# Retention and two gated layers on one core: Lo parts of x and the first twelve weight tiles' additions moved from VectorE to GpSimd

## The chip, the cores and the metric

The kernel runs on one core of a Trainium2 chip. Its engines are TensorE (PE, with PEld for its weight loads), VectorE (DVE), ScalarE (ACT), GpSimd (POOL) and SyncE (SP), which issues most DMAs. Each engine works through its own instructions in order and waits on semaphores for the others. The metric is the device time of one execution in microseconds; less is better.

## What is computed

Retention over 4 batches, 8 heads, 576 positions and head size 64, then a layer with a clipped square, then a layer with a product of two branches:

```python
scores = scale * np.matmul(q, k.transpose(0, 1, 3, 2))
ret = scores * Dmat[None]            # Dmat: gamma ** (i - j) below the diagonal
x = np.matmul(ret, v)                # to 2304 tokens x 512
h = x @ moe_w_in                     # 512 x 2048
g = np.where(h >= 1, h, np.where(h <= -1, 0.0, (h + 1) ** 2 / 4))
x = g @ moe_w_out                    # 2048 x 512
out = ((x @ w_a) * (x @ w_b)) @ w_out  # 512 x 1536, 512 x 1536, 1536 x 512
```

The weights are float64 in memory.

## The kernel before

Most matmuls take operands in a 32-bit form of their own (float32r). To keep accuracy, x, g and every weight tile are held as two parts: Hi is a copy in that form, made by ScalarE, and Lo is the difference between the value and Hi, made by VectorE. A product is three matmuls, Hi by Hi, Hi by Lo, Lo by Hi (`HL`).

The retention runs in 36 units u, two for each chunk of 128 tokens. A unit's data come by one DMA from SP (L379) into a tile `u`, of which four exist, so unit u's load waits until unit u - 4 has been used by TensorE. GpSimd multiplies its values by a decay (L387) and, for a chunk in which a sequence begins, clears a part (L390, memset). TensorE makes scores (`s`), VectorE masks them (`retf`, L417), TensorE makes the output (`po`) and the state (`pn`), VectorE scales the output into `xf` (L481), ScalarE copies Hi into `x` (L486) and VectorE writes Lo into `x` (L487). The first 14 units use plain float32 operands; the later ones are split in Hi and Lo as well (`z` L395/L396, `ret` L425/L426, `st` L472/L473).

Six units make one block of 384 tokens. From block 0 on, the first layer runs in steps: a step is a column chunk f of w_in (`ph`, twelve matmuls of 128x384, L523 on), the activation (`act1`: `t` L535 to L537, `g` L541/L542) and the product with the row chunk f of w_out into four accumulators (`acc`). While block b runs its steps, one unit or more of block b + 1 is done in each step. Steps go in three groups of chunks (`GROUPS1`); in the first group block 0 uses chunks 0 to 3 and blocks 1 to 5 use 0 to 5, so that twelve weight tiles, w_in and w_out of chunks 0 to 5, are needed there. The groups' sums are stored (`yst`, L577, by VectorE and ScalarE in turn, then a DMA from SP) and added to later. x is stored too (`xd`, L939), by SP.

A weight tile comes as raw 64-bit words (`raw`, L140, by SP's queue until about 84 us, by GpSimd's after that) and is converted in place of a cast: two ScalarE instructions (L152, L153), a shift (L154), a merge of the sign (L157) and an integer addition (L160) on VectorE give `conv`. Then `split` (L163) writes Hi (L165, ScalarE) and Lo (L166, VectorE) into `w`. `conv` has two buffers, `raw` three and one more in the early part. `made[0]` counts the tiles of the first layer that are done, 32 in all.

The program is recorded in source order, and a scheduler then sets the order of each engine's instructions by a timeline of its own. So an edit to a few lines can move others on every engine. The second layer (`qx`, `qy`, `qz`, `late`) converts its weights by the same functions, with `made[0]` past 12.

Of the kernel before, what the change touches and what calls it, by code (L numbers as in the profile page):

```python
# [9 lines left out]
F32 = mybir.dt.float32  # L10
# [5 lines left out]
ALU = mybir.AluOpType  # L16
# [9 lines left out]
    [(0, 4)] + [(0, 6)] * (NB1 - 1), [(4, 11)] + [(6, 11)] * (NB1 - 1), [(11, 16)] * NB1  # L26
]
WHOLE = 14
NF2 = 12
HT = 384  # L30
WBUFS, WBUFS2 = 17, 1
# [50 lines left out]
def retention_ffn_kernel(  # L82
# [12 lines left out]
    nc = tc.nc  # L95
# [31 lines left out]
    def col_chunk(w, f):  # L127
        return w[:, f * P:(f + 1) * P].rearrange("(c p) f -> p c f", p=P)
# [14 lines left out]
    def convert(raw, t=None):  # L143


        w = raw.bitcast(U32).rearrange("p (n t) -> p t n", t=2)
        low, high = w[:, 0, :], w[:, 1, :]
        r = raw.bitcast(I32).rearrange("p (n t) -> p t n", t=2)[:, 0, :]
        if t is None:
            t = cpool.tile([P, 512], F32, tag="conv", name="conv")  # L150
        tu, ti = t.bitcast(U32), t.bitcast(I32)
        nc.scalar.activation(t, high.bitcast(F32), AF.Abs, scale=2.0 ** -112)  # L152
        nc.scalar.activation(r, low, AF.Copy, scale=2.0 ** -29)  # L153
        nc.vector.tensor_scalar(  # L154
            out=tu, in0=tu, scalar1=3, scalar2=None, op0=ALU.logical_shift_left
        )
        nc.vector.scalar_tensor_tensor(  # L157
            out=tu, in0=high, scalar=0x80000000, in1=tu, op0=ALU.bitwise_and, op1=ALU.bitwise_or
        )
        nc.vector.tensor_tensor(out=ti, in0=ti, in1=r, op=ALU.add)  # L160
        return t

    def split(t, pool):  # L163
        wt = pool.tile([P, 2, 512], F32R, tag="w", name="w")
        nc.scalar.copy(wt[:, 0, :], t)  # L165
        nc.vector.tensor_sub(wt[:, 1, :], t, wt[:, 0, :].bitcast(F32))  # L166
        return wt


# [10 lines left out]
    second = []  # L180
    for p in range(NF2 // 2):
        if p == LEAD:
            second += [row_chunk(w_out2, f) for f in range(2)]
        second += [col_chunk(w, 2 * p + j) for w in (w_a, w_b) for j in range(2)]
    second += [row_chunk(w_out2, f) for f in range(2, NF2)]
    weights, home = {}, {}
    room = {"w": [wpool, WBUFS]}
    made = [0]
# [55 lines left out]

    qd = [[dpool.tile([P, 2, 512], F32, name=f"q{p}_{k}") for k in range(7)] for p in range(NF2 // 2)]
    od = [[dpool.tile([P, 2, 512], F32, name=f"o{j}_{r}") for r in range(NF2 // 4)] for j in range(7)]
    A11, A12, A21, A22, S1, S2, S3, S4 = range(8)
# [3 lines left out]
    def maker():  # L251

        for p in range(NF2 // 2):
            if p == LEAD:
                yield from last_tiles(0, 2)
            tiles = {}
            for w in range(2):
# [24 lines left out]
                yield  # L282
        yield from last_tiles(2, NF2)

# [96 lines left out]
    def prepare(u):  # L381
# [7 lines left out]
        if more:  # L389
            nc.gpsimd.memset(t[0:r0, R0:V0], 0.0)  # L390
        if u < WHOLE:
            units[u, "z"] = t.unsqueeze(1)
# [8 lines left out]
    def passes(u):  # L401

        return HL[:1] if u < WHOLE else HL

    def score(u):
# [14 lines left out]
        )  # L420
        if u < WHOLE:
            rets[u] = f.unsqueeze(1)
# [10 lines left out]
    def output(u):  # L433
        c, d = divmod(u, 2)
        z, r = units[u, "z"], rets.pop(u)
# [5 lines left out]
        for e in range(2):  # L441
# [6 lines left out]
            for r0, _, m in inter:  # L448
                st = state[d].unsqueeze(1) if u < WHOLE else split_state[d]
                for n, (a, b) in enumerate(hl):  # L450
# [6 lines left out]
        if s0 + m < S:  # L457
# [10 lines left out]
            else:  # L468
                nc.vector.tensor_add(st, pn[:, 0:2 * P], st)
            if u + 2 >= WHOLE:  # L470
                h = split_state[d] = a2.tile([P, 2, 2 * P], F32R, tag=f"st{d}", name="st")
# [5 lines left out]
        fv = f.rearrange("p (c i) -> p c i", c=2)  # L477
# [6 lines left out]
            )  # L484
        xs = x[:, :, 2 * d:2 * d + 2, o]
        cast[0] = nc.scalar.copy(xs[:, 0], fv)  # L486
        nc.vector.tensor_sub(xs[:, 1], fv, xs[:, 0].bitcast(F32))  # L487
        del units[u, "z"]

    masked, cast = [None], [None]  # L490
# [584 lines left out]
```

## Time and profile before

| what | us |
|---|---|
| median of 3 runs | 926.08 (924.2 to 927.02) |
| the profiled execution | 925.54 |
| its span, first to last instruction | 923.8 |
| TensorE busy in it | 906.6 |
| VectorE busy | 662.0 |
| ScalarE busy | 486.3 |
| GpSimd busy | 69.9 |

TensorE's mean granted clock is 0.995 of 2.4 GHz. Busy times are sums over the span; the share of an engine differs much between the early part, where weights are converted and units run beside the first layer, and the rest. A matmul's row lists a duration that overlaps its neighbours', since they are pipelined; the pace is the difference between starts.

### The profile page before, as it was taken

The page shows a single profiled execution, that of the slowest core. Times are in us where ns is not written, and L with a number is a line of the kernel's source. Part 1 is how long each engine was busy: PE and PEld are TensorE (multiplying, and loading weights), DVE is VectorE, ACT ScalarE, POOL GpSimd, SP SyncE. Part 2 cuts the span into 40 slices and gives each one's busy share as a digit, 9 for nine tenths or more (in the row PEclk, how much of TensorE's full clock was granted, in tenths as well). Part 3 has the DMA queues.
Part 4 walks back from the last instruction along what each step waited for, and adds up shares of the span by engine and source line. Part 5 has one row for each costly group of instructions (what it writes and reads, how often), then busy time and mean ns, then how long its engine had stood idle before and what let it go on. Part 6 is the DMA issues. An engine that isn't in the chain of part 4 may idle for free.

```text
span 923.8 us, 14702 instructions
## 1 busy us (share of the span) xinstructions
PE 906.6 (98%) x5324; PEld 897.1 (97%) x5324; DVE 662.0 (72%) x1242; ACT 486.3 (53%) x961; POOL 69.9 (8%) x104
## 2 busy tenths in 40 slices
PE   6999999999999999999999999999999999999998
PEld 5889989999999999999999999999999999999998
DVE  4999888887788989698876877775554476255465
ACT  2565555655777667676755555453333254233243
POOL 1112021000021111011100000000000000000000
PEclk8999999999999999999999999999999999999999
DMA  9867344440688998799995998879954589966483
GB/s 357 297 207 285 117 185 148 145 169 3 239 296 288 384 358 279 273 343 401 400 405 200 370 409 309 284 237 320 332 180 159 160 263 384 367 198 223 155 294 149
DMA packets 81097, 244.14 MB, mean 264 GB/s; under 512 B 8417, under 2 KB 35169, under 8 KB 78593
## 3 DMA queue, kind: packets, MB, share of 16 engines
q1 hardware_dynamic: 71952, 210.01, 63.4%
q0 software_dynamic: 8928, 33.03, 10.0%
q8 instruction: 42, 0.69, 0.3%
q14 instruction: 31, 0.25, 0.1%
q10 hardware_dynamic: 144, 0.17, 0.1%
HBM read 181.83 MB, written 61.34 MB: 263 GB/s over the span
## 4 chain that ended last, share of the span: by engine, by line
PE 90%; DVE 5%; DMA 3%; issue 1%; ACT 0%; SPq 0%; ACTq 0%
PE acc L114 31%; PE ph L114 20%; PE qx L114 16%; PE qy L114 8%; PE late L114 4%; PE qz L114 4%; PE po L114 3%; DMA u<-in_qkv 2%; PE s L114 2%; PE pn L114 1%; DMA y<-yst 1%; DVE conv L160 1%; DVE conv L157 1%; DVE xf L481 1%; DVE w L166 1%
## 5 line engine op out<-in xcount | busy, mean ns | idle before, releaser
L114 PE MATMUL acc<-g,w 128*128 128x384 f32 x1296 | 249.4, 336 | 1.9 <-ACT yst L577 1.5
L114 PEld LDWEIGHTS acc<-g,w 128*128 128x128 f32 x1296 | 225.7, 188 | 2.7 <-ACT yst L577 1.9
L114 PE MATMUL ph<-x,w 128*128 128x384 f32 x1152 | 219.2, 336 | 1.4 <-ACT w L165 1.2
L114 PEld LDWEIGHTS ph<-x,w 128*128 128x128 f32 x1152 | 200.7, 188 | 2.3 <-ACT w L165 1.3
L114 PE MATMUL qx<-tx,w 128*128 128x384 f32 x864 | 165.5, 334 | 0.0
L114 PEld LDWEIGHTS qx<-tx,w 128*128 128x128 f32 x864 | 151.2, 188 | 0.0
L657 ACT COPY keep<-qx 128x384 f32<-128x384 f32 x126 | 59.8, 480 | 136.8 <-PE qx L114 130.8
L114 PE MATMUL qy<-tx,w 128*128 128x384 f32 x432 | 86.5, 334 | 0.0
L114 PE MATMUL acc<-sp,w 128*128 128x384 f32 x432 | 77.5, 334 | 0.0
L114 PEld LDWEIGHTS qy<-tx,w 128*128 128x128 f32 x432 | 75.9, 188 | 0.0
L114 PEld LDWEIGHTS acc<-sp,w 128*128 128x128 f32 x432 | 75.1, 188 | 0.0
L537 DVE SCALAR_TENSOR_TENSOR t<-t,ph 128x384 f32<-128x384 f32 x96 | 52.6, 550 | 23.8 <-ACT t L536 23.6
L541 ACT CAST g<-t 128x384 fp32r<-128x384 f32 x96 | 48.8, 510 | 38.1 <-DVE t L537 37.5
L535 ACT ACTIVATE t<-ph 128x384 f32<-128x384 f32 x96 | 46.6, 486 | 40.0 <-PE ph L114 39.5
L542 DVE TENSOR_TENSOR g<-t,g 128x384 fp32r<-128x384 f32 x96 | 53.4, 558 | 13.7 <-ACT g L541 13.6
L153 ACT ACTIVATE raw<-raw 128x512 int32<-128x512 uint32 x68 | 45.9, 675 | 22.8 <-DMA raw<-in_moe_w_a 7.9
L750 DVE TENSOR_TENSOR sp<-gb,sp 128x768 fp32r<-128x768 f32 x42 | 40.2, 957 | 22.1 <-ACT sp L749 21.9
L749 ACT CAST sp<-gb 128x768 fp32r<-128x768 f32 x42 | 35.2, 837 | 32.7 <-PE acc L114 18.8
L536 ACT ACTIVATE t<-t 128x384 f32<-128x384 f32 x96 | 50.3, 525 | 1.7
L692 DVE TENSOR_TENSOR keep<-keep 128x384 f32<-128x384 f32 x36 | 20.0, 557 | 39.6 <-ACT keep L657 39.6
L679 DVE TENSOR_TENSOR keep<-qz,keep 128x384 f32<-128x384 f32 x36 | 20.0, 557 | 33.1 <-PE qz L114 32.2
L114 PE MATMUL qz<-tx,w 128*128 128x384 f32 x216 | 43.4, 334 | 0.0
(107 smaller groups left out, 1213.9 us busy)
## 6 DMA issues: line engine op xcount, KB each, us to landing
w<-q SPq DMA_DIRECT2D x126, 512.0 KB, 6.0
u<-in_qkv SPq DMA_DIRECT2D x36, 640.0 KB, 4.7
q<-q SPq DMA_DIRECT2D x42, 512.0 KB, 7.1
w<-o SPq DMA_DIRECT2D x42, 512.0 KB, 4.7
x<-xd SPq DMA_DIRECT2D x12, 1536.0 KB, 9.3
raw<-in_moe_w_out POOLq DMA_DIRECT2D x21, 512.0 KB, 6.7
xd<-x SPq DMA_DIRECT2D x6, 1536.0 KB, 7.1
yin<-y SPq DMA_DIRECT2D x48, 192.0 KB, 5.6
```

Of the source, the lines that this page charges most:

```text
L114: nc.tensor.matmul(o, l, r, start=start, stop=stop, skip_group_check=goes_on)
L153: nc.scalar.activation(r, low, AF.Copy, scale=2.0 ** -29)
L535: nc.scalar.activation(t, ph[:, :TB], AF.Relu, bias=0.5, scale=0.5)
L536: nc.scalar.activation(t, t, AF.Square)
L537: nc.vector.scalar_tensor_tensor(out=t, in0=t, scalar=1.0, in1=ph[:, :TB], op0=ALU.min, op1=ALU.max)
L541: nc.scalar.copy(g[:, 0, :], t),
L542: nc.vector.tensor_sub(g[:, 1, :], t, g[:, 0, :].bitcast(F32)),
L657: nc.scalar.copy(t, o[:, :HT])
L679: nc.vector.tensor_add(self.c11, z[:, :HT], self.c11)
L692: nc.vector.tensor_add(self.c22, self.c22, self.s5)
L749: nc.scalar.copy(t[:, 0], b)
L750: nc.vector.tensor_sub(t[:, 1], b, t[:, 0].bitcast(F32))
```

## The change

Three instructions change engine, under a new constant `EARLY = 12`. The Lo part of x (L487) is made by GpSimd for all 36 units. The integer addition that ends a conversion (L160) and the Lo part of a weight tile (L166) are made by GpSimd while `made[0]` is under 12, which is the twelve tiles named above; the other 20 tiles, and all tiles of the second layer, stay on VectorE. What is computed is the same.

```diff
--- before.py
+++ after.py
@@ -26,6 +26,7 @@
     [(0, 4)] + [(0, 6)] * (NB1 - 1), [(4, 11)] + [(6, 11)] * (NB1 - 1), [(11, 16)] * NB1
 ]
 WHOLE = 14
+EARLY = 12
 NF2 = 12
 HT = 384
 WBUFS, WBUFS2 = 17, 1
@@ -157,13 +158,17 @@
         nc.vector.scalar_tensor_tensor(
             out=tu, in0=high, scalar=0x80000000, in1=tu, op0=ALU.bitwise_and, op1=ALU.bitwise_or
         )
-        nc.vector.tensor_tensor(out=ti, in0=ti, in1=r, op=ALU.add)
+        (nc.gpsimd if made[0] < EARLY else nc.vector).tensor_tensor(
+            out=ti, in0=ti, in1=r, op=ALU.add
+        )
         return t
 
     def split(t, pool):
         wt = pool.tile([P, 2, 512], F32R, tag="w", name="w")
         nc.scalar.copy(wt[:, 0, :], t)
-        nc.vector.tensor_sub(wt[:, 1, :], t, wt[:, 0, :].bitcast(F32))
+        (nc.gpsimd if made[0] < EARLY else nc.vector).tensor_sub(
+            wt[:, 1, :], t, wt[:, 0, :].bitcast(F32)
+        )
         return wt
 
 
@@ -484,7 +489,7 @@
             )
         xs = x[:, :, 2 * d:2 * d + 2, o]
         cast[0] = nc.scalar.copy(xs[:, 0], fv)
-        nc.vector.tensor_sub(xs[:, 1], fv, xs[:, 0].bitcast(F32))
+        nc.gpsimd.tensor_sub(xs[:, 1], fv, xs[:, 0].bitcast(F32))
         del units[u, "z"]
 
     masked, cast = [None], [None]
```

GpSimd's order around units 6 to 10. Before, it has one multiply for each unit (`u_287` is unit 6, `u_422` is unit 10) and two memsets:

```order
L387 TENSOR_TENSOR u_287<-u_287,con_156 128x256
L387 TENSOR_TENSOR u_320<-u_320,con_156 128x256
L387 TENSOR_TENSOR u_342<-u_342,con_156 128x256
L390 MEMSET u_342 64x256
L387 TENSOR_TENSOR u_393<-u_393,con_156 128x256
L390 MEMSET u_393 64x256
L387 TENSOR_TENSOR u_422<-u_422,con_156 128x256
```

After, Lo parts of x (`x_226` is block 0, `x_410` is block 1), additions (`conv_364` is the third tile, `conv_375` the fourth) and Lo parts of weights (`w_370` the third tile, `w_381` the fourth) stand between them:

```order
L392 TENSOR_TENSOR u_342<-u_342,con_156 128x256
L395 MEMSET u_342 64x256
L492 TENSOR_TENSOR x_226<-xf_359,x_226 128x2x128
L161 TENSOR_TENSOR conv_364<-conv_364,raw_263 128x512
L392 TENSOR_TENSOR u_393<-u_393,con_156 128x256
L395 MEMSET u_393 64x256
L161 TENSOR_TENSOR conv_375<-conv_375,raw_318 128x512
L169 TENSOR_TENSOR w_370<-conv_364,w_370 128x512
L492 TENSOR_TENSOR x_410<-xf_411,x_410 128x2x128
L169 TENSOR_TENSOR w_381<-conv_375,w_381 128x512
L492 TENSOR_TENSOR x_410<-xf_440,x_410 128x2x128
L392 TENSOR_TENSOR u_422<-u_422,con_156 128x256
```

Where each multiply waited for its load alone, other work now stands in front of it and behind it in one queue.

VectorE's order at the fifth and sixth tile (`conv_453`, `conv_464`), before:

```order
L157 SCALAR_TENSOR_TENSOR conv_464<-raw_384,conv_464 128x512
L417 TENSOR_TENSOR retf_489<-s_486,con_156 128x512
L537 SCALAR_TENSOR_TENSOR t_511<-t_511,ph_475 128x384
L160 ISA conv_453<-raw_373,conv_453 128x1024
L160 ISA conv_464<-raw_384,conv_464 128x1024
L481 TENSOR_TENSOR xf_500<-po_491,con_156 64x256 x2
L467 COPY state0_157<-pn_496 128x256
L542 TENSOR_TENSOR g_512<-t_511,g_512 128x384
L166 TENSOR_TENSOR w_459<-conv_453,w_459 128x512
L166 TENSOR_TENSOR w_470<-conv_464,w_470 128x512
L487 TENSOR_TENSOR x_410<-xf_500,x_410 128x2x128
L417 TENSOR_TENSOR retf_569<-s_566,con_156 128x512
```

and after, from the same merge to the same mask:

```order
L158 SCALAR_TENSOR_TENSOR conv_464<-raw_384,conv_464 128x512
L422 TENSOR_TENSOR retf_489<-s_486,con_156 128x512
L542 SCALAR_TENSOR_TENSOR t_511<-t_511,ph_475 128x384
L486 TENSOR_TENSOR xf_500<-po_491,con_156 64x256 x2
L547 TENSOR_TENSOR g_512<-t_511,g_512 128x384
L472 COPY state0_157<-pn_496 128x256
L155 TENSOR_SCALAR conv_534<-conv_534 128x512
L158 SCALAR_TENSOR_TENSOR conv_534<-raw_462,conv_534 128x512
L422 TENSOR_TENSOR retf_569<-s_566,con_156 128x512
```

Five instructions are gone between the two masks (two additions, two Lo parts of weights, one of x), and the next tile's shift and merge have moved in.

TensorE's order at the seventh tile, `w_540`, behind the `pn` of unit 10, before:

```order
L114 MATMUL pn_604<-u_422 128x128 x2
L114 MATMUL ph_632<-x_226,w_540 128x384 x2
L114 MATMUL s_642<-u_563 128x256 x2
L114 MATMUL acc0_518<-g_614,w_470 128x384 x2
L114 MATMUL acc1_519<-g_614,w_470 128x384 x2
L114 MATMUL acc2_520<-g_614,w_470 128x384 x2
L114 MATMUL acc3_521<-g_614,w_470 128x384 x2
L114 MATMUL ph_632<-x_226,w_540 128x384 x10
```

and after:

```order
L115 MATMUL pn_604<-u_422 128x128 x2
L115 MATMUL ph_632<-x_226,w_540 128x384 x12
L115 MATMUL s_642<-u_563 128x256 x2
L115 MATMUL acc0_518<-g_614,w_470 128x384 x2
L115 MATMUL acc1_519<-g_614,w_470 128x384 x2
L115 MATMUL acc2_520<-g_614,w_470 128x384 x2
L115 MATMUL po_647<-retf_597,u_482 128x256
```

The twelve ph matmuls on that tile are no longer cut after two; all stand ahead of the next scores and of acc.

## Rows read from the trace of the kernel before

**Rows 1.** Busy us (instructions) by stretch: PE, PEld, DVE, ACT, POOL; PEclk, DMA share, GB/s

```profile
30.00:90.00 60.00, 57.62 (x328) 53.59 (x327) 59.39 (x114) 37.30 (x70) 11.52 (x16) 1.00 0.79 284
90.00:130.00 40.00, 37.78 (x252) 36.92 (x252) 32.76 (x56) 22.30 (x40) 5.78 (x6) 1.00 0.47 159
130.00:240.00 110.00, 110.00 (x745) 109.93 (x744) 88.07 (x159) 60.85 (x112) 8.52 (x14) 1.00 0.37 129
240.00:923.80 683.80, 678.92 (x3915) 678.02 (x3913) 465.49 (x883) 358.03 (x726) 39.37 (x58) 1.00 0.80 288
sum 923.80, PE 906.63 PEld 897.14 DVE 661.98 ACT 486.28 POOL 69.89; mean PE 181.33 PEld 179.43 DVE 132.40 ACT 97.26 POOL 13.98
```

**Rows 2.** Waits of PE, 30 to 130 us: us in total, times, longest us

```profile
PE acc L114 <- ACT yst L577: 1.5, 1, 1.5
PE ph L114 <- ACT w L165: 1.2, 1, 1.2
PE pn L114 <- DVE t L537: 0.8, 2, 0.6
PE s L114 <- DVE z L396: 0.5, 1, 0.5
PE acc L114 <- ACT g L541: 0.3, 1, 0.3
PE ph L114 <- DVE retf L417: 0.2, 1, 0.2
```

**Rows 3.** Chain that ended last: start us, us, what

```profile
56.50 1.62 DVE conv L160 x2
...
88.24 2.08 PE ph L114 x12
```

**Rows 4.** DVE groups from 30 to 90 us: busy us, mean ns | idle before

```profile
L160 DVE CUSTOM_DVE_ANT_0 conv<-raw,conv 128x1024 uint16<-128x1024 uint16 x11 | 9.0, 832 | 0.0
...
L166 DVE TENSOR_TENSOR w<-conv,w 128x512 fp32r<-128x512 f32 x11 | 7.8, 722 | 0.0
L157 DVE SCALAR_TENSOR_TENSOR conv<-raw,conv 128x512 uint32<-128x512 uint32 x10 | 7.1, 727 | 0.1
...
L396 DVE TENSOR_TENSOR z<-u,z 128x1280 fp32r<-128x1280 f32 x3 | 4.4, 1483 | 0.0
L487 DVE TENSOR_TENSOR x<-xf,x 128x256 fp32r<-128x256 f32 x10 | 4.1, 415 | 0.0
...
L542 DVE TENSOR_TENSOR g<-t,g 128x384 fp32r<-128x384 f32 x6 | 3.7, 609 | 0.1
```

**Rows 5.** POOL in order of time: start us, us, line, operation [idle before <-releaser]

```profile
20.64 0.61 POOL L387 TENSOR_TENSOR u<-u,con 128x256 f32<-128x256 f32 x1 [8.43 <-DMA u<-in_qkv]
...
32.60 0.61 POOL L387 TENSOR_TENSOR u<-u,con 128x256 f32<-128x256 f32 x1 [1.79 <-DMA u<-in_qkv]
...
37.68 0.61 POOL L387 TENSOR_TENSOR u<-u,con 128x256 f32<-128x256 f32 x1 [4.22 <-PE ph L114]
38.23 0.30 POOL L390 MEMSET u<- 64x256 f32 x1
...
73.78 1.94 POOL L387 TENSOR_TENSOR u<-u,con 128x256 f32<-128x256 f32 x1 [1.49 <-DMA u<-in_qkv]
```

**Rows 6.** DVE in order of time, two additions of weight tiles

```profile
35.34 0.69 DVE L160 CUSTOM_DVE_ANT_0 conv<-raw,conv 128x1024 uint16<-128x1024 uint16 x1
...
37.77 1.07 DVE L160 CUSTOM_DVE_ANT_0 conv<-raw,conv 128x1024 uint16<-128x1024 uint16 x1
```

**Rows 7.** PE in order of time

```profile
26.21 0.59 PE L114 MATMUL po<-retf,u 128*128 128x256 f32 x2
...
40.19 2.32 PE L114 MATMUL ph<-x,w 128*128 128x384 f32 x12 [0.24 <-DVE retf L417]
...
57.08 0.61 PE L114 MATMUL pn<-u 128*128 128x128 f32 x4
58.87 0.59 PE L114 MATMUL ph<-x,w 128*128 128x384 f32 x2 [1.19 <-ACT w L165]
```

## The prediction

> **What bounds the kernel now.** I read the busy time by stretch first, then TensorE's waits, then VectorE's groups, then single rows. TensorE is busy for 906.6 of the 923.8 us [rows 1], so at most 17.2 us of the span are open to any change. By stretch, 2.4 us of that lie between 30 and 90 us, 2.2 us between 90 and 130, none from 130 to 240, and 4.9 us after 240 us, where the moved instructions are over. The 7.7 us that are left lie before 30 us, where the kernel loads and no moved instruction is waited for. So the change can be worth 4.6 us by this view, although it takes about 20 us of work from VectorE.
>
> VectorE is what is full in the early stretch: 59.39 of the 60 us from 30 to 90, with GpSimd at 11.52 [rows 1]. TensorE's waits from 30 to 130 us [rows 2] add to 4.5 us in six lines. Five end on VectorE's work or on ScalarE work that follows it (1.2 for a weight tile's Hi part, 0.8 for t, 0.5 for z, 0.3 for g, 0.2 for retf: 3.0 us). The sixth, 1.5 us for yst, ends on a copy that follows a DMA. The chain shows the first of them being made: 1.62 us of two additions at L160 stand in it at 56.5 [rows 3], the weight's Hi part comes after them, and TensorE, which has issued its last pn at 57.08, starts the ph on that tile at 58.87 [rows 7].
>
> **What leaves VectorE.** From 30 to 90 us: eleven additions (9.0 us), eleven Lo parts of weights (7.8) and ten Lo parts of x (4.1), 20.9 us [rows 4]. That is a third of the stretch, so VectorE is no longer full and the instructions behind the moved ones come earlier. The order on VectorE shows it: two additions and two Lo parts no longer stand between a t and the next retf.
>
> **What GpSimd gets.** A two-input instruction of 128x256 takes 0.61 us there [rows 5]. So a Lo part of x costs 0.61. A Lo part of weights, 128x512, is twice that, 1.22 us. The integer addition has no row on GpSimd: from below it costs the 0.69 us that VectorE needs for it when nothing disturbs it [rows 6], from above four times the 0.61, 2.44 us, if it is handled as the 1024 half-words that VectorE's form lists [rows 4]. I take 1.22, as for the other 128x512 instruction, since its size is nearest to that row. The sum for 30 to 90 us is then 13 u and 10 x at 0.61, and 22 instructions at 1.22: 14.0 + 26.8 = 40.9 of 60 us. GpSimd has the room.
>
> The Trainium skill, GPSIMD Engine Reference, section 3.1, gives 4497 ns for an addition of 2048 float elements on GpSimd; an estimate from that page for 512 elements is a quarter, 1.12 us. By it the sum would be 38.7 us in place of 40.9. No row here shows an integer addition on that engine.
>
> **What the two engines share.** Three rows say that they hold each other up. The u multiply at 73.78 took 1.94 us instead of 0.61 while VectorE ran the Lo part of z, and the addition at 37.77 took 1.07 us on VectorE instead of 0.69 while GpSimd ran a u multiply at 37.68 [rows 5, 6]. Both are instructions with two operands in SBUF. So the work does not simply vanish beside VectorE: VectorE's own two-operand instructions that stay (L157 7.1, z 4.4, g 3.7 us [rows 4], 15.2 together) and GpSimd's 40.9 take turns, 56.1 of 60 us. That still fits, but with 4 us of room, and single instructions will be stretched on both sides. VectorE's other instructions (xf, retf, state, t read PSUM) run beside it.
>
> This is the rule of the Trainium skill, SBUF — State Buffer, section "Who interferes with whom": a VectorE instruction with two SBUF inputs and a GpSimd instruction that reads SBUF exclude each other, and the second waits for the whole of the first. The trace agrees, with 1.94 us for 0.61. It speaks against this change, and its result is the slower rival below.
>
> **Where the new queue costs.** GpSimd works in order, and u multiplies wait for their loads, so whatever stands behind one waits too. I go through the places.
> - Start: three x parts and one tile now stand ahead of the multiply at 20.64 [rows 5], 3 x 0.61 + 2 x 1.22 = 4.3 us. If none of it began sooner, the multiply would start at 24.9 and end at 25.6; its reader on TensorE starts at 26.21 [rows 7]. Hidden.
> - x of the sixth unit stands behind the multiply at 32.60 and a memset: 32.60 + 0.61 + 0.30 + 0.61 = 34.1. VectorE made it in a full stretch too, and only the second half of the first ph reads it; hidden.
> - The third weight tile's Lo part stands behind the multiply at 37.68, its memset (ends 38.53 [rows 5]) and an addition of the next tile: 38.53 + 1.22 + 1.22 = 40.97. It is read by the third matmul of the ph that starts at 40.19 [rows 7]. Twelve such matmuls take 2.08 us [rows 3], 0.17 each, so that one issued at 40.54. This is 0.43 us late: the 0.2 us wait for retf at that place is replaced by this.
> - The seventh tile, for which TensorE waits at 58.87: from 40.97 GpSimd has 3 x, 2 u and 6 tile instructions to do up to its addition, 5 x 0.61 + 6 x 1.22 = 10.4 us, so 51.3 if no input is late. TensorE is there at 57.7 (57.08 + 0.61). That is 6 us of cover. At 2.44 for each addition, four of them (one before 40.97) take 4.9 us more, and 1.5 is left.
>
> After 90 us GpSimd has an x part for every unit beside a u multiply, and each u that stands ahead landed before. After 240 us nothing moved runs; only the scheduler's order differs, and I cost it at nothing, with 1 us either way.
>
> **The sum.** Of the waits, 1.2 (weight), 0.8 (t) and 0.3 (g) go with VectorE's backlog; of the 0.5 for z I count half, since that instruction stays and is of the sort that GpSimd holds up: 2.55 us. The 1.5 for yst stays, being behind a DMA. Less 0.43 for the third tile: 2.1 us. Against the profiled execution's own time, 925.54 (span 923.8 and 1.74 around it), that is 923.4. The median of the runs shown, 926.08, is 0.54 above that execution, so the forecast is 924.0.
>
> **Rivals.**
> 1. The whole of the waits goes, yst too: if x is complete earlier, its store to xd goes out earlier, and the y stores behind it in SP's queue as well. 926.08 - 4.5 = 921.6. For it: TensorE's waits in this stage are in their majority VectorE's. Against: the 1.5 us belongs to the DMA, and the shared turn makes new waits. The gaps between starts are some 0.17 us longer than the waits listed (57.69 to 58.87 hides the modelled end), six times 0.17 is 1 us more: 920.6.
> 2. The shared turn fills up, and the change is slower. Place: 30 to 90 us. Turn time is 56.1 us with additions at 1.22; eleven additions fill the last 3.9 us when they cost 0.35 more, so the point from which it decides is 1.57 us for an addition. At 2.44 it is 69.5 us, 9.5 too many. The last four tiles are not read before block 1's fifth step, so part of that delays nobody; with half, 4.8 us, the time is 930.9, with all 935.6. For it: there is no row of that addition on GpSimd. Against: 1.57 is more than twice VectorE's price.
> 3. Nothing changes, as TensorE's small waits move to other places of the same size: 926.08. It lies in the same class as the forecast.
>
> **How the numbers follow.** A measurement of this kernel tells about 0.3% from no change, 2.8 us, so 923.3 to 928.9 is "within". Forecast and rival 3 (within): 0.44, the forecast alone 0.3. Rival 1 (faster): 0.33. Rival 2 (slower): 0.23. The range for 8 in 10 takes in rival 1 with its further 1 us, 920.0 rounded down, and rival 2 at half its price, 931.0; left out are its full price and an unlucky order later on.
>
> **What would show it.** VectorE from 30 to 90 us at 38 to 48 us busy instead of 59.4, and GpSimd near 41. Additions on GpSimd at 1.2 us where nothing disturbs them; over 1.57, rival 2. The wait of 1.2 us for a weight's Hi part gone, and one of some 0.4 us for a weight's Lo part on GpSimd at the second ph. The yst wait still there. The forecast is wrong if TensorE's waits between 30 and 130 us add to less than 1.5 us or more than 5, or if the time after 240 us changes by more than 1 us.

## The result: slower by two thirds of a per cent

The changed kernel takes 931.24 us (median of 6 runs, 930.59 to 932.18), the kernel before 924.47 on the same chip (6 runs): 6.8 us more by the medians; the ratio is 1.0064 with a 95% interval of 1.0054 to 1.0074, which is 5.9 us. Where kernels are compared below, the ratios are used. The prediction said 924.0 us, within 0.3%, and a range up to 931.0. The time lies just above that range, on the side of the slower rival. The forecast was a gain of 2.1 us from a base of 926.08, the median of three runs; the sign is wrong, whichever base is taken.

The profiled execution took 930.73 us, its span 928.9, 5.1 more than before. The first view is the busy time by stretch, in the columns of [rows 1].

```profile
30.00:90.00 60.00, 55.36 (x312) 50.66 (x310) 50.33 (x75) 34.14 (x64) 47.77 (x47) 1.00 0.79 283
90.00:130.00 40.00, 37.98 (x249) 37.47 (x250) 33.83 (x52) 23.98 (x45) 11.61 (x12) 1.00 0.43 146
130.00:240.00 110.00, 108.99 (x742) 108.73 (x742) 88.36 (x145) 61.53 (x112) 26.15 (x29) 1.00 0.36 123
240.00:928.90 688.90, 683.74 (x3939) 682.17 (x3937) 468.93 (x887) 358.06 (x729) 40.47 (x60) 1.00 0.80 288
```

From 30 to 90 us TensorE is idle for 4.64 us instead of 2.38, from 130 to 240 for 1.01 instead of none. VectorE's busy time (third pair) falls from 59.39 to 50.33 us, so 20.9 us of work left it and only 9.1 us went. GpSimd has 47.77 us instead of 11.52.

TensorE's waits, to be laid beside [rows 2] (us in total, times, longest us). The view is of the whole span; ret and ScalarE's g lie behind 130 us, the others between 30 and 130. Two longer ones at its top, which lie outside and which the kernel before has too, are left out:

```profile
...
PE ph L115 <- DVE t L542: 1.9, 1, 1.9
PE po L115 <- DVE ret L431: 1.0, 1, 1.0
PE s L115 <- DVE t L542: 1.0, 1, 1.0
PE acc L115 <- DVE g L547: 0.9, 1, 0.9
PE s L115 <- DVE z L401: 0.9, 1, 0.9
PE acc L115 <- ACT g L546: 0.8, 2, 0.5
PE po L115 <- DVE xf L486: 0.8, 2, 0.4
PE po L115 <- DVE state L474: 0.8, 1, 0.8
...
```

The waits for a weight tile's Hi part and for yst are gone under these names. In their place stand waits that end on instructions that VectorE kept: t, g, z, xf, state. Two of them are not of VectorE's making. The longest is the 1.9 us for a t at 91 us: VectorE stood idle for 2.65 us before it, because ScalarE, which begins each t, stood still for 3.04 us until a store of y had landed. `t` and `yst` share one pool of buffers, so a t can wait for a store. ScalarE, then SP:

```profile
89.05 0.96 ACT L540 ACTIVATE t<-ph 128x384 f32<-128x384 f32 x2 [3.04 <-DMA y<-yst]
```
```profile
79.63 3.65 SPq L586 DMA_DIRECT2D y<-yst  x4
```

In the kernel before the first of these stores left at 75.55 and no t waited for one. The 0.8 us for state at 79.7 stands behind a z, for which ScalarE waited 3.39 us for a u multiply on GpSimd; the load of that u had landed at 70.36, and it began at 75.33, behind GpSimd's new work. For the waits on t at 62 us and on g and xf, VectorE's groups from 30 to 90 us say why (columns as in [rows 4]; L158 is the merge that was L157, L155 the shift that was L154, L547 the Lo part of g). First the shift and xf in the kernel before, then the changed kernel:

```profile
L481 DVE TENSOR_TENSOR xf<-po,con 64x256 f32<-64x256 f32 x20 | 8.4, 418 | 0.1
...
L154 DVE TENSOR_SCALAR conv<-conv 128x512 uint32<-128x512 uint32 x10 | 4.5, 461 | 0.0
```
```profile
L158 DVE SCALAR_TENSOR_TENSOR conv<-raw,conv 128x512 uint32<-128x512 uint32 x10 | 13.3, 1335 | 0.2
L486 DVE TENSOR_TENSOR xf<-po,con 64x256 f32<-64x256 f32 x18 | 7.5, 418 | 1.2 <-PE po L115 1.1
L155 DVE TENSOR_SCALAR conv<-conv 128x512 uint32<-128x512 uint32 x10 | 7.5, 747 | 1.5 <-ACT conv L153 1.4
L422 DVE TENSOR_TENSOR retf<-s,con 128x512 f32<-128x512 f32 x10 | 6.8, 684 | 0.8 <-PE s L115 0.6
L547 DVE TENSOR_TENSOR g<-t,g 128x384 fp32r<-128x384 f32 x5 | 5.1, 1024 | 0.0
```

The merge grew from 727 to 1335 ns, the shift from 461 to 747, g from 609 to 1024. What reads PSUM did not change: xf and retf stand at 418 and 684 ns (before 418 and 681). GpSimd's groups of the same stretch:

```profile
L169 POOL TENSOR_TENSOR w<-conv,w 128x512 fp32r<-128x512 f32 x11 | 15.6, 1418 | 0.1
L161 POOL TENSOR_TENSOR conv<-conv,raw 128x512 int32<-128x512 int32 x11 | 14.9, 1357 | 5.0 <-DVE conv L158 1.8 <-POOL conv L161 1.4 <-ACT raw L154 1.1
L492 POOL TENSOR_TENSOR x<-xf,x 128x256 fp32r<-128x256 f32 x10 | 9.1, 914 | 0.4 <-ACT x L491 0.2
L392 POOL TENSOR_TENSOR u<-u,con 128x256 f32<-128x256 f32 x12 | 8.5, 710 | 6.7 <-DMA u<-in_qkv 6.0 <-PE s L115 0.5 <-PE ph L115 0.2
```

One of the new waits in order of time, first VectorE, then GpSimd (start us, us, engine, line, operation):

```profile
60.01 1.67 DVE L158 SCALAR_TENSOR_TENSOR conv<-raw,conv 128x512 uint32<-128x512 uint32 x1
61.59 0.54 DVE L542 SCALAR_TENSOR_TENSOR t<-t,ph 128x384 f32<-128x384 f32 x1
```
```profile
59.63 1.48 POOL L169 TENSOR_TENSOR w<-conv,w 128x512 fp32r<-128x512 f32 x1
```

The merge starts while GpSimd makes the Lo part of a weight tile (until 61.11). It takes 1.67 us, an undisturbed one 0.68, and behind it stands the t for which TensorE waits 1.0 us. At 69.10 the same happens to g, which takes 1.63 us beside another weight Lo part, and TensorE waits 0.9.

### The profile page after: what moved, and what is told of

Its sections match the earlier page's. It is cut to its first block, busy times and chain, and to the rows that moved or that the text cites. A ratio compares the mean times of both kernels' runs of the same rounds, so it can differ in the third digit from the quotient of the medians.

```text
span 928.9 us, 14732 instructions
## 1 busy us (share of the span) xinstructions
PE 907.8 (98%) x5324; PEld 896.9 (97%) x5324; DVE 654.5 (70%) x1182; ACT 485.0 (52%) x961; POOL 136.9 (15%) x164
## 4 chain that ended last, share of the span: by engine, by line
PE 67%; DMA 1%; ACT 0%; DVE 0%; issue 0%
PE acc L115 23%; PE qx L115 16%; PE ph L115 11%; PE qy L115 8%; PE late L115 4%; PE qz L115 4%; DMA raw<-in_moe_w_a 1%; ACT raw L154 0%; ACT g L546 0%; ACT q L279 0%; DVE keep L718 0%; ACT ost L845 0%; ACT t L541 0%; ACT t L540 0%
## 5 line engine op out<-in xcount | busy, mean ns | idle before, releaser
L547 DVE TENSOR_TENSOR g<-t,g 128x384 fp32r<-128x384 f32 x96 | 56.6, 592 | 12.3 <-ACT g L546 12.1
L154 ACT ACTIVATE raw<-raw 128x512 int32<-128x512 uint32 x68 | 45.8, 675 | 20.3 <-DMA raw<-in_moe_w_out 6.6
L754 ACT CAST sp<-gb 128x768 fp32r<-128x768 f32 x42 | 35.2, 837 | 32.7 <-PE acc L115 18.8
L492 POOL TENSOR_TENSOR x<-xf,x 128x256 fp32r<-128x256 f32 x36 | 37.8, 1050 | 51.3 <-ACT x L491 48.1
```

The source lines that it names most:

```text
L492: nc.gpsimd.tensor_sub(xs[:, 1], fv, xs[:, 0].bitcast(F32))
L547: nc.vector.tensor_sub(g[:, 1, :], t, g[:, 0, :].bitcast(F32)),
L754: nc.scalar.copy(t[:, 0], b)
```

## The experiments

Two theories stood against each other: that the instructions which GpSimd received and those which VectorE kept hold each other up, and that the scheduler, which gave all engines a new order, gave them a worse one. In some kernels the order of PE, ScalarE, VectorE and SyncE is held to that of another kernel by a table of instruction numbers; a moved instruction drops out of it, GpSimd's own order stays free, and line numbers grow by some twenty. To compare profiles I add, from the starts of the matmuls, how far each step from one to the next exceeds the usual step of its form. The busy view models ends and catches less of this. Each row is one execution, and a wait that spans 90 us counts on one side of it only. In us:

| kernel | 0-30 | 30-90 | 90-130 | 130-450 | behind | sum |
|---|---|---|---|---|---|---|
| before | 8.7 | 4.4 | 3.4 | 2.1 | 1.9 | 20.5 |
| changed | 9.6 | 7.9 | 1.9 | 4.9 | 1.9 | 26.2 |
| changed, order of before | 10.0 | 7.3 | 1.6 | 2.5 | 1.8 | 23.2 |
| before, order of changed | 9.3 | 7.4 | 5.8 | 4.5 | 1.9 | 28.8 |
| x only, new order | 9.4 | 6.4 | 3.6 | 4.8 | 1.9 | 26.0 |
| x only, order of before | 10.0 | 5.7 | 1.6 | 3.8 | 1.9 | 22.8 |
| weights only, new order | 9.9 | 9.5 | 2.2 | 2.5 | 1.9 | 26.0 |
| weights only, order of before | 8.5 | 8.8 | 1.5 | 3.5 | 1.9 | 24.1 |

The column from 0 to 30 holds the waits for the first loads; it differs by over 1 us between kernels with the same order there, so a difference of 1 us there means nothing. Of the 5.7 us by which the changed kernel's sum exceeds that of before, 2.0 lie between 30 and 130 us, where the moved instructions crowd, and 2.8 between 130 and 450.

### The order alone, both ways

```diff
+ORDER = "..."
+def keep_order(tc, nc):
...
+        for a, b in zip(names, names[1:]):
+            tc.add_manual_dep(
+                here[b], a,
...
+        keep_order(tc, nc)
```

> The changed kernel, with the instructions of TensorE, VectorE, ScalarE and SyncE held in the order that the kernel before has; only GpSimd's own order is left to the scheduler. Theory 1 (the two engines hold each other up at SBUF): the loss stays, 928 to 934 us, with the sign merges on VectorE at 1.2 us or more in the mean from 30 to 90 us. Theory 2 (the new order of the other engines, the y stores and TensorE's early ph above all, makes the loss): 922 to 926 us, even with the merges stretched.

Measured: 926.97 us against 924.09, ratio 1.0028 (1.0018 to 1.0039), span 925.7. With the order of before the same moves cost 2.6 us instead of 5.9, counted by the ratios. So 0.36%, 3.3 us, is the new order's (the medians, 931.24 and 926.97, would say 4.3), and the spans, 928.9 and 925.7, differ by 3.2. The wait for a t at 91 us behind a store of y is of this part: in the order of before no t waits for a store, and in the next kernel, which has the new order and nothing moved, ScalarE waits 3.51 us for one and TensorE 2.5 behind it. Another place where it is seen is 165 us. VectorE in the changed kernel, then with the order of before:

```profile
162.42 1.82 DVE L401 TENSOR_TENSOR z<-u,z 128x1280 fp32r<-128x1280 f32 x1
164.16 1.01 DVE L582 COPY yst<-acc 128x384 f32<-128x384 f32 x2
165.10 0.41 DVE L478 TENSOR_TENSOR st<-state,st 128x256 fp32r<-128x256 f32 x1
165.43 0.68 DVE L431 TENSOR_TENSOR ret<-retf,ret 128x512 fp32r<-128x512 f32 x1
```
```profile
161.54 0.69 DVE L451 TENSOR_TENSOR ret<-retf,ret 128x512 fp32r<-128x512 f32 x1
162.26 1.02 DVE L602 COPY yst<-acc 128x384 f32<-128x384 f32 x2
163.20 1.56 DVE L421 TENSOR_TENSOR z<-u,z 128x1280 fp32r<-128x1280 f32 x1
```

In the new order ret stands behind z and two copies of y, and TensorE waits 1.0 us for it; in the old one it comes first and no wait appears. Neither z nor ret was touched by the change.

The 2.6 us that stay are not the order's. From 30 to 90 us the merge still takes 933 ns, the shift 613, g 1190, and the Lo part of st (state and its Hi part, both in SBUF) 2132 instead of 410. The longest of these holds, VectorE first, then GpSimd:

```profile
86.37 3.23 DVE L498 TENSOR_TENSOR st<-state,st 128x256 fp32r<-128x256 f32 x1
89.52 0.54 DVE L562 SCALAR_TENSOR_TENSOR t<-t,ph 128x384 f32<-128x384 f32 x1
```
```profile
86.75 0.76 POOL L512 TENSOR_TENSOR x<-xf,x 128x256 fp32r<-128x256 f32 x1
87.45 0.62 POOL L412 TENSOR_TENSOR u<-u,con 128x256 f32<-128x256 f32 x1
88.02 1.28 POOL L189 TENSOR_TENSOR w<-conv,w 128x512 fp32r<-128x512 f32 x1
```

The st begins while GpSimd issues a load (85.82 to 86.73), and three GpSimd instructions in a row run before it ends: 3.23 us for what takes 0.41. Then TensorE waits 1.2 us for the t behind it. Another st, held to 1.04 us at 79.73, is followed by a wait of 1.6 us for a t (0.6 at this place before). Not all of the 2.6 us is located: in the table this kernel exceeds the one before by 1.1 us between 30 and 130 us and by 0.4 from 130 to 450; the rest of the difference lies in the first column.

> The kernel before (all three kinds of instructions on VectorE), with TensorE, VectorE, ScalarE and SyncE held in the order that the changed kernel has. Theory 1 (sharing at SBUF): 923 to 927 us, no loss, as nothing new runs on GpSimd. Theory 2 (order): 928 to 933 us.

Measured: 931.82 us, ratio 1.0073 (1.0059 to 1.0087). The old assignment in the new order is as slow as the changed kernel, as the second theory said. So within the new order the moves cost nothing: 0.64% with them, 0.73% without. The split into 3.3 us for the order and 2.6 for the sharing is the one that is found in the order of before, and the two don't add. At 62.8 us TensorE waits for the same t as in the changed kernel, 1.25 us, here behind an addition that stayed on VectorE. This run is less clean than the first, since the new order was made for a VectorE with less to do, and it had the old load here (56.86 us from 30 to 90 us). The execution profiled is also the slowest of its five, 933.52 us, and lost some 1.7 us to the clock, which was at 0.50 to 0.88 from 92 to 98 us, right behind TensorE's wait of 2.5 us.

### The two halves of the change, in both orders

```diff
-EARLY = 12
+EARLY = 0
```

> Only the Lo parts of x go to GpSimd (EARLY = 0); the scheduler orders anew. Theory 1: 10 instructions of 0.7 us from 30 to 90 us take 7 us of shared time for 4 us given back by VectorE, a third of the change's load: 924 to 928 us, at most a third of the loss. Theory 2: whatever its order brings, 922 to 933.

Measured: 929.53 us, ratio 1.0053 (1.0040 to 1.0066), above the first theory's 924 to 928. VectorE is at 57.77 us from 30 to 90, GpSimd at 22.08.

```diff
-        nc.gpsimd.tensor_sub(xs[:, 1], fv, xs[:, 0].bitcast(F32))
+        nc.vector.tensor_sub(xs[:, 1], fv, xs[:, 0].bitcast(F32))
```

> Only the additions and Lo parts of the first twelve weight tiles go to GpSimd; x stays on VectorE; the scheduler orders anew. Theory 1: 22 instructions of 1.3 us from 30 to 90 us, four fifths of the new load on GpSimd: most of the loss, 927 to 932 us. Theory 2: whatever its order brings, 922 to 933.

Measured: 930.54 us, ratio 1.0066 (1.0053 to 1.0078). So each half alone costs nearly what both cost. The same two kernels with the order of before:

> The x Lo parts alone on GpSimd (the weights' Lo and addition stay on VectorE), with PE, ScalarE, VectorE and SyncE held in the order of before. Theory 1 (two prices: the new order of all engines some 4 us, the sharing between GpSimd and VectorE some 3 us): no price of order here, and of the 48 us that GpSimd gains in 30 to 90 us only some 12, so a quarter of the sharing's 3 us less the little that VectorE gives up: 924 to 925.5, the merge (scalar_tensor_tensor of conversion) at 750 to 830 ns in 30 to 90 us against 727 before. Theory 2 (the x Lo parts on GpSimd are late themselves, whatever the order): as with the scheduler's order, 928.5 to 930.5. Theory 3 (sharing is nothing, the weights' late pieces are all): 923 to 924, merge at 727.

Measured: 926.82 us, ratio 1.0024 (1.0011 to 1.0036), by its median above the first theory's 924 to 925.5. The new order costs the x half 0.29%, 2.7 us. Of 4.1 us that left VectorE [rows 4] nothing is to be seen there: it stays at 59.31 us, because w's Lo part takes 903 ns instead of 722, the merge 833, the shift 553.

> Lo and addition of the first twelve weight tiles on GpSimd, the x Lo parts on VectorE, in the order of before. Theory 1 (sharing): merge 900 to 960 ns and shift 600 to 770 ns in 30 to 90 us as in the two kernels that moved the weights, TensorE's excess over its usual pace in 60 to 90 us 4 us or more against 1.6 before, 926 to 927.5. Theory 2 (the whole is the order): 923 to 924.5, excess in 60 to 90 us as before. Theory 3 (both pieces together fill GpSimd and only then does it cost): 924 to 925.

Measured: 930.09 us, ratio 1.0061 (1.0048 to 1.0075), well above all that I expected. Against the same kernel in the new order the difference is 0.05%, with intervals that nearly coincide, so an effect of the order is not seen here, and what GpSimd received makes the loss. It is not all VectorE being held: 1.2 us of TensorE's waits are for a weight's Lo part that is late on GpSimd itself. The listed clocks, 0.992 to 0.998 against 0.995 to 0.998 for the kernel before, put some 1.3 of the 5.6 us down to the clock (an estimate from the mean clock and span of every run). The merge, 795 ns, and the shift, 468, are held up less than I expected, another group of VectorE more:

```profile
L512 DVE TENSOR_TENSOR x<-xf,x 128x256 fp32r<-128x256 f32 x10 | 13.4, 1340 | 2.0 <-ACT x L511 2.0
```

The x Lo parts, left on VectorE, take 1340 ns instead of 415 beside the weights on GpSimd, 13.4 us instead of 4.1. That would explain why moving the weights alone is worse than moving both: x moved along takes ten held instructions off VectorE. The weight half's price is therefore mostly GpSimd's new load, the x half's mostly the order, and the two don't add.

### Work on GpSimd that nobody reads

A third theory is that only pieces which GpSimd delivers late matter. To see the sharing without any moved piece, the kernel before keeps its assignment and its order, and GpSimd gets idle work behind each u multiplication of units 7 to 16. `EXTRA` holds the names of the added instructions, which the table of the order must skip.

```diff
-        nc.gpsimd.tensor_mul(v, v, dec)
+        mul = nc.gpsimd.tensor_mul(v, v, dec)
+        if 7 <= u < 17:
+            with tc.issue_after(mul.ins):
+                for _ in range(2):
+                    EXTRA.add(nc.gpsimd.tensor_tensor(
+                        out=junk, in0=con[:, 0:512], in1=con[:, 512:1024], op=ALU.add
+                    ).ins.name)
```

> The kernel before in its own order, with nothing moved; behind each u multiplication of units 7 to 16 GpSimd makes two additions of 128x512 out of the constants into a tile that nobody reads (20 in all, two SBUF operands each, some 25 us on GpSimd in 30 to 90 us). Theory 1 (instructions with two SBUF operands on the two engines hold each other up): merge, g and addition on VectorE longer by 15 to 40%, the merge at 830 to 1000 ns against 727; VectorE was full (59.4 of 60 us), so TensorE waits: 927 to 932. Theory 2 (only who makes which piece, and its lateness, matters): 923.5 to 925, merge at 727.

Measured: 943.43 us, ratio 1.0203 (1.0190 to 1.0216), more than either theory had. VectorE's groups from 30 to 90 us (addition, shift, xf):

```profile
L187 DVE CUSTOM_DVE_ANT_0 conv<-raw,conv 128x1024 uint16<-128x1024 uint16 x9 | 10.2, 1149 | 0.0
...
L515 DVE TENSOR_TENSOR xf<-po,con 64x256 f32<-64x256 f32 x17 | 7.1, 418 | 0.1
L181 DVE TENSOR_SCALAR conv<-conv 128x512 uint32<-128x512 uint32 x9 | 6.8, 770 | 0.0
```

The addition takes 1149 ns instead of 832, the shift 770 instead of 461, xf as ever 418. Part of the 18.8 us is TensorE's clock. Three stretches of four us (columns as in [rows 1]):

```profile
38.00:42.00 4.00, 1.98 (x11) 1.55 (x9) 3.97 (x4) 0.24 (x1) 3.88 (x5) 1.00 1.02 344
42.00:46.00 4.00, 1.97 (x5) 1.64 (x6) 3.96 (x8) 2.44 (x6) 0.88 (x2) 0.65 0.87 290
46.00:50.00 4.00, 4.00 (x14) 3.64 (x13) 3.99 (x5) 1.35 (x4) 2.57 (x3) 0.50 0.52 160
```

TensorE was busy for half of 38 to 46 us, then the granted clock went to 0.50, which is 1.2 GHz, although it was busy without a break from 46 on. Over all stretches of four us with less than 1.00 up to 102 us, what is missing adds to 8.5 us; some 10 us are left for the waits themselves. In the profiled execution of the changed kernel the clock stayed at 1.00 from 30 us on, so its loss holds nothing of this.

```diff
-                for _ in range(2):
-                    EXTRA.add(nc.gpsimd.tensor_tensor(
-                        out=junk, in0=con[:, 0:512], in1=con[:, 512:1024], op=ALU.add
-                    ).ins.name)
+                for _ in range(9):
+                    EXTRA.add(nc.gpsimd.memset(junk[:, 0:256], 0.0).ins.name)
```

> The same with nine memsets of 128x256 in place of the two additions: GpSimd is as busy but reads nothing. Theory 1 (sharing comes from two operands read out of SBUF): merge at 720 to 760 ns, 923.5 to 925.5. Rival (any work of GpSimd on SBUF holds VectorE up, writing too): as with the additions, merge at 830 to 1000 ns and 927 to 932. Where reads and writes both change nothing, sharing is not the cause and the lateness of the pieces on GpSimd is.

Measured: 926.18 us, ratio 1.0019 (1.0010 to 1.0028), 0.7 us above the first theory's bound. From 30 to 90 us GpSimd is busy for longer than with the additions (39.70 against 34.53 us). The groups of GpSimd, then of VectorE:

```profile
L419 POOL MEMSET junk<- 128x256 f32 x90 | 29.2, 324 | 4.6
```
```profile
L184 DVE SCALAR_TENSOR_TENSOR conv<-raw,conv 128x512 uint32<-128x512 uint32 x10 | 7.5, 768 | 0.1
L193 DVE TENSOR_TENSOR w<-conv,w 128x512 fp32r<-128x512 f32 x11 | 7.4, 683 | 0.0
```

w's Lo part is shorter than before (683 against 722 ns) and the merge 41 ns longer in the mean: two of the ten, beside u multiplies, took 1.10 us, and the other eight, five of them beside memsets, 0.68 to 0.69. The shift, of one operand, is touched by memsets: where the two met, the shift took up to 623 ns instead of some 420, the memset 471 to 513 instead of 311, or both. So 29 us of GpSimd's time that only writes cost a tenth of what the twenty additions cost, and less than a fifth of it without the clock's part. Where the 1.8 us lie the profile of this kernel doesn't show: its span is 924.1.

```diff
+                for _ in range(4):
+                    EXTRA.add(nc.gpsimd.tensor_copy(out=junk, in_=con[:, 0:512]).ins.name)
```

> The kernel before in its own order with four copies of 128x512 from the constants to a tile that nobody reads behind each u multiplication of units 7 to 16 (40 in all, one SBUF operand read and one written, in place of the 20 additions with two operands read). Theory 1 (only instructions that read two SBUF operands hold the other engine up): as with the memsets, 924 to 927, w Lo on VectorE at 680 to 750 ns, merge at 720 to 780 ns. Rival (whatever GpSimd reads from SBUF holds VectorE up): w Lo 900 ns or more, the time 930 to 943, nearer to the 943.4 of the additions.

Measured: 929.84 us, ratio 1.0054 (1.0037 to 1.0071): neither theory, between both. GpSimd, then VectorE, from 30 to 90 us:

```profile
L419 POOL COPY junk<-con 128x512 f32<-128x512 f32 x24 | 22.1, 921 | 0.7
```
```profile
L193 DVE TENSOR_TENSOR w<-conv,w 128x512 fp32r<-128x512 f32 x10 | 8.3, 849 | 0.0
...
L184 DVE SCALAR_TENSOR_TENSOR conv<-raw,conv 128x512 uint32<-128x512 uint32 x10 | 7.9, 810 | 0.1
...
L181 DVE TENSOR_SCALAR conv<-conv 128x512 uint32<-128x512 uint32 x10 | 5.2, 538 | 0.0
```

One operand read on GpSimd is enough to lengthen VectorE's two-operand instructions and the shift; my theory that GpSimd's must read two as well is wrong. A copy takes 0.61 us undisturbed and 0.92 here.

> One addition of 128x512 in place of two behind each u multiplication of units 7 to 16 (10 in all, some 13.6 us on GpSimd). If the price is by the instruction and VectorE has no slack: half of the 19 us that 20 additions cost, 932 to 935. If VectorE can hide the first turns and only what goes beyond costs (what the prediction assumed of the shared turns): 925 to 928.

The kernel is that of the two additions with one instead. Measured: 931.91 us, ratio 1.0075 (1.0054 to 1.0095). Ten additions of 1.27 us each cost 6.9 us. The execution profiled, in which the granted clock stayed at 1.00 from 30 us on, is the fastest of the six, 927.98 us; the other five took 931.00 to 933.75 at a mean clock of 0.993 to 0.994 instead of 0.997. By the mean clocks of all runs some 1.7 of the 6.9 us are the clock's, which leaves some 5.2, half of the 10 us that are left of the 18.8. So VectorE did not hide the first turns.

### Half of the order

> The changed kernel with each engine held in the order of before for all that before ran up to 132 us, and the scheduler free behind that. If the 4 us that the new order costs (931.2 against 927.0 in the order of before) arise early, at the waits of 56 and 91 us: 926.5 to 928, TensorE's excess over its usual pace in 130 to 450 us 2.5 us or less. If they arise late (the wait for ret at 165 us, for g at 293 and 307 us): 929.5 to 931.5, excess 130 to 450 us near the 4.9 of the changed kernel.

The edit is the first one, with the table cut off behind 132 us. Measured: 927.84 us, ratio 1.0038 (1.0022 to 1.0053).

> The mirror: the scheduler free for the first 132 us and the order of before held for the rest. If the price of the order arises early: 930 to 931.5, with the wait of 2 us for the copies of y at 91 us still there. If late: 927 to 928.5, the waits at 165, 293 and 307 us gone. If the two halves each give back about half, the price is no single place's: both near 929.

The table's other part. Measured: 928.46 us, ratio 1.0045 (1.0027 to 1.0062). Each half gives back some 2 us (0.26 and 0.19%) of the 3.3. The intervals overlap, so neither half is told from the other, and the order's price is not one place's: the second kernel still has the wait of 1.8 us for t at 91 us, again behind a store of y, and lost those at 165, 293 and 307; the first lost the ones at 91 and 165, waits 1.25 us for t at 89 behind an st held for 3.22 us, and still for g at 291 and 305 us.

### GpSimd's own reading taken away

```diff
-        nc.gpsimd.tensor_mul(v, v, dec)
+        if 7 <= u < 17:
+            for h in range(4):
+                mul = nc.scalar.activation(
+                    v[:, h], v[:, h], AF.Copy,
+                    scale=kdec[:, c % places, 4 * d + h:4 * d + h + 1],
+                )
+                if h:
+                    EXTRA.add(mul.ins.name)
+        else:
+            nc.gpsimd.tensor_mul(v, v, dec)
```

> The kernel before in its own order, but the u multiplications of units 7 to 16 go from GpSimd to ScalarE (four instructions of 128x64 each, a per-partition factor instead of the broadcast), so that GpSimd reads nothing in most of 30 to 90 us. Theory 1 (reading by GpSimd stretches VectorE's instructions, and the kernel before pays for it already): VectorE's addition and Lo of the conversion fall from 832 and 722 ns to 690 to 720, some 2 to 3 us of VectorE come free of 59.4, and with ScalarE having 22 us to spare there, 921.5 to 924. Theory 2 (the stretch matters only through pieces that GpSimd delivers late): no change, 923.5 to 925, if ScalarE's added 10 to 12 us find room; above 925.5 if they delay its casts of g and w.

Measured: 925.43 us against 924.83, ratio 1.0008 (1.0000 to 1.0017). VectorE's groups from 30 to 90 us are now undisturbed:

```profile
L187 DVE CUSTOM_DVE_ANT_0 conv<-raw,conv 128x1024 uint16<-128x1024 uint16 x11 | 7.5, 696 | 0.0
L193 DVE TENSOR_TENSOR w<-conv,w 128x512 fp32r<-128x512 f32 x11 | 7.4, 688 | 0.0
...
L184 DVE SCALAR_TENSOR_TENSOR conv<-raw,conv 128x512 uint32<-128x512 uint32 x10 | 6.7, 685 | 0.1
...
L181 DVE TENSOR_SCALAR conv<-conv 128x512 uint32<-128x512 uint32 x10 | 4.1, 422 | 0.9 <-ACT conv L179 0.7
```

VectorE is busy for 56.87 us instead of 59.39, as the first theory said, but the time did not fall. ScalarE has 45.01 us instead of 37.30, and the wait of 1.2 us for a weight's Hi part [rows 7] is there again, longer: TensorE starts the ph behind it at 60.46, just after ScalarE ends a Hi part at 60.41. So this run does not bear out that the kernel before could be made faster this way, which the first theory expected.

## Why the prediction was wrong, point by point

**What bounds it.** That TensorE's waits, and not VectorE's load, limit the gain was right: 9.1 us less on VectorE brought none. The wait for a weight's Hi part went, as predicted. That the yst wait stays was wrong by its name and right in kind: at its old place TensorE no longer waits for it, and a wait of 1.9 us for another store of y, through a t, has come up at 91 us.

**GpSimd's price per instruction was right.** I took 1.22 us for an addition and for a weight's Lo part, 0.61 for x. Undisturbed they take 1.27, 1.27 and 0.72 us in the changed kernel. The point from which the slower rival was to decide, 1.57 us for an addition, was not reached: its mean is 1.36.

**The step that failed first is the shared turn: "That still fits, but with 4 us of room".** Instead of a gain of 2.1 us the moves cost 2.6 with the order of before held. I counted the merge, z and g on VectorE's side and left out the shift. The shift reads one operand in SBUF, and [rows 5, 6] had shown me two-operand instructions alone. But beside the changed GpSimd it takes 747 ns, and 422 where GpSimd reads nothing, so it takes turns too. With undisturbed durations and the counts of [rows 4] the turn from 30 to 90 us is: on GpSimd 22 x 1.27 + 10 x 0.72 + 13 x 0.61 = 43.1; on VectorE 10 x 0.685 (merge) + 10 x 0.42 (shift) + 3 x 1.48 (z) + 6 x 0.55 (g) = 18.8. That is 61.9 of 60 us in place of 56.1, and the sum says "full" without any dear addition. The Lo parts of st and ret, two of each here, have two SBUF operands as well and are in neither sum; with them it is 64, and an st is the instruction that was held longest. So rival 2's mechanism came true at the price that was to exclude it. The Trainium skill, SBUF — State Buffer, section "Who interferes with whom", says of `tensor_scalar` that it too can take the pair of ports that VectorE shares with GpSimd, in a two-port mode, and that two-input instructions contend with GpSimd's reads but not with what only writes. The trace agrees in all three: 747 ns for the shift, 1335 for the merge, and 0.68 to 0.69 us for the five merges that ran beside memsets alone. I had used half of that rule. The prediction's form of it, that the second waits for the whole of the first, was too mild for the st above: it waited through three.

Worked out in the same way, with the addition at 0.70, w's Lo part at 0.69 and x's at 0.42 where they stay on VectorE, and with the idle instructions that fall into this stretch (19 of the twenty additions, 24 of the forty copies), the price of the kernels that run in the order of before goes up with the turn in the main:

| kernel | turn of 60 us | price by the ratio, us |
|---|---|---|
| u multiplications on ScalarE | 40 | 0.7 |
| before | 46 | 0 |
| before and ninety idle memsets | 46 | 1.8 |
| x only | 49 | 2.2 |
| weights only | 59 | 5.6, some 1.3 of it by the clock |
| before and ten idle additions | 59 | 6.9, some 1.7 of it by the clock |
| before and forty idle copies | 61 | 5.0 |
| the whole change | 62 | 2.6 |
| before and twenty idle additions | 70 | 18.8, some 8.5 of it by the clock |

The whole change is cheaper than its turn says. What would explain it, and was not tried by itself, is that VectorE has less to do: a held instruction comes on top of VectorE's own work, and only there were 10 us free to take it (49.5 us busy from 30 to 90, against 55.3 with the weights alone). Both have to be added up then, the turn and VectorE's load. And a single stretched merge in front of a t or a g makes TensorE wait at once, whatever room there is later.

**The second step that failed is "only the scheduler's order differs, and I cost it at nothing, with 1 us either way".** It is worth 3.3 of the 5.9 us (by the ratios) with the whole change and 2.7 with x alone, and it lies on both sides of 132 us. For the time before 240 us the prediction has no term for the order at all, beyond its places in GpSimd's queue. With nothing moved the new order alone costs 6.7 us, 0.73%, so by itself it would account for the whole loss. The places that are known are the t behind a store of y at 91 us, 1.9 us, and ret at 165 us, 1.0. TensorE's excess from 130 to 450 us rose by 2.8 us, where no wait names GpSimd. The prediction's condition for being wrong, waits above 5 us between 30 and 130, came true as well: they add to 6.6.

**Smaller terms.** At the start 24.9 + 0.61 is 25.5 and not 25.6, which changes nothing. The third tile's Lo part, 0.43 us late by my sum, is in no wait; at 38 us TensorE waits for VectorE's xf instead, behind a held merge. The gain of 2.55 us on w, t, g and half of z became: w 1.2 gained, t from 0.8 to 2.9, of which 1.9 is the store of y, g from 0.3 to 0.9, z from 0.5 to 0.9. What came first behind VectorE's backlog was freed, and what stands behind a held merge, or is held itself, was not. My list of places in GpSimd's queue lacked the u multiply that began at 75.33, 5 us after its load, and through z and state cost TensorE 0.8 us. Of VectorE's busy time, 50.3 us where I had 38 to 48, merge and shift alone took back 9.2.

**What stays open.** Which swaps in the new order cost what, beyond ret at 165 us and the t at 91. The two half kernels in the order of before wait some 0.8 us at 296 and 297 us for g behind a conversion whose load came late; the whole change in the same order waits for the same load and not for that g, and why is not known. The price of sharing with the order held (0.28% for both halves, 0.61% for weights alone) was measured, not derived.

## What to carry to other kernels

Moving elementwise work from a full VectorE to an idle GpSimd frees little where both read SBUF: add up, with undisturbed durations, every VectorE instruction with two SBUF operands and every single-operand one that may use the shared ports, beside all that GpSimd will read, and look at what stands right behind a held one. GpSimd work that only writes cost little here (1.8 us for 29), and VectorE work that reads PSUM beside its second operand was not held. Where a pool of buffers serves both a work tile and a tile that waits to be stored, ask for which store the work tile would wait in the new order. Where a scheduler orders all engines, a small move is two changes, and holding the old order shows what the move costs without the second.

## What the runs showed of the hardware that I had not expected

- A single-operand shift on VectorE, 128x512, takes 422 ns with GpSimd not reading and 747 to 770 beside its reads.
- GpSimd copies with one operand hold VectorE up (w's Lo part 849 ns against 683 beside memsets). Memsets left the merge alone and held the shift, up to 623 ns instead of some 420.
- One VectorE instruction can be held through several of GpSimd's: a 128x256 subtraction of 0.41 us took 3.23 beside three in a row.
- Two GpSimd instructions of the same shape, 128x256 with two operands, take 0.61 us (u) and 0.72 (x's Lo part) undisturbed. Why wasn't tried.
- Twenty idle additions on an engine that was mostly idle cost 18.8 us, the largest effect of all runs, some 8.5 of them by TensorE's clock, which fell as low as 0.50, 1.2 GHz, after its waits.
